# A recurrence with a top-2 mixture of experts: routing in two groups of twelve tiles instead of three of eight

## The chip, the core and the metric

One Trainium2 chip; the kernel runs on one core of it. The time is that of one execution on the device in microseconds (us). Before the change: 607.7 us, the median of three runs (606.4 to 608.46). The core has five engines that run their own instruction queues in order: TensorE (PE, with its weight loads PEld), VectorE (DVE), ScalarE (ACT), GpSimd (POOL) and SyncE (SP, here the queue that issues most DMAs).

## The reference

```python
# 1. recurrence per batch (4) and head (8), 768 steps, 48 dims
for t in range(S):
    cur = einsum('bhd,bhe->bhde', u[None] * kt, vt)
    y[:, :, t] = einsum('bhd,bhde->bhe', rt, state + cur)
    state = w[None, :, :, None] * state + einsum('bhd,bhe->bhde', kt, vt)
# 2. x: [3072 tokens, 384]; gate
noisy = x @ w_gate + log1p(exp(x @ w_noise)) * noise          # [3072, 8]
top2  = the two largest of each row; weights = softmax over the two
# 3. eight experts, 384 -> 1024 -> 384, float32
out[mask] += top2_w * (maximum(x[mask] @ w1[e], 0) @ w2[e])
```

## The kernel before, in words

**Stage 1, the recurrence ("attention"), 24 tiles.** A tile i is 128 tokens of one batch. For each tile, SP loads k, r and v (192 KB each, 1,024 rows of 192 bytes), POOL multiplies k by its decay table and makes r*k*u, PE turns k and r (`turn_kr`), multiplies them (`scores`), DVE masks the result (`mask`, L450), PE makes the output (`yout`, L496), and DVE adds the u term (`xout`, L522). That add, one per tile, is called x(i) below; it ends a tile. SP then writes x to DRAM (`xd`), from where experts gather their tokens by row. SP's queue is in order: the write of x(i) stands ahead of the loads of k and r for tile i+6, and those are issued five tiles ahead of use (`load(i + 5, (0, 2))`). Into the same loop go the loads of the noise (`load_nz`, four, 24 KB each in rows of 32 bytes, iterations 1 to 4) and the weights of expert 0 (seven units, three of 512 KB and four of 384 KB, at the iterations of the table `W_LD`), each of which ACT and DVE then split into a high and a low part (L344 to L349).

**Routing.** The gate of a group of tiles is worked out by `route(g)`, a generator of some sixty small DVE steps: softplus by polynomials, top-2 by two maxima, ranks within the experts by PE (L771 to L774), gate weights (written to `xd` as extra columns, L802), and then the list of expert 0's tokens. The lists are made by PE: `drop` builds two one-hot matrices on DVE (`r_oa`, `r_ob`), `place` multiplies them (L661), `placed` adds the result to `L`; `rows` turns it into row numbers `GR` (L819 to L821), by which POOL gathers (`xgather`, L956). Groups are 8 tiles. In the tile loop `steps(n)` takes n steps of the oldest generator at fixed places of each iteration, seven in all; so an order written out by hand decides which routing step stands where in DVE's queue. After the loop `rstep(us)` does the same between matmuls, with a credit in us.

**Stage 2, the experts.** Each expert has 832 token slots, seven tiles t (the last of 64 rows). Experts 1 to 7 take them in two chunks, tiles 0 to 2 (384 rows) and 3 to 6 (448 rows). `p1` makes the hidden layer (eight blocks f of nine matmuls, float32 in three products of high and low parts, L1053; ACT and DVE write `hb`), `p2` the output tile by tile (24 matmuls each, L1087). Expert 0 starts while routing is not finished, in three chunks: tiles 0 and 1 (256 rows) hold tokens of the first eight tiles only, tiles 2 and 3 those of the next eight, tiles 4 to 6 the rest. So the list of the first chunk is made in the tile loop (`early(0)`, at iteration 21), that of the second while PE works on the first (`list_01`, `early(1)`), and so on; the transposes of a chunk's gathered rows (`xT`, L979) stand in PE's queue inside `p2` of the chunk before it. Expert 1 needs all three groups (`list_1`), whose lists are made during expert 0's last chunk.

The change touches the tables at L47 and L48, L81, L84, L90, L92, `uterm_b` and `uterm_c`, `logits_out`, `drop`, `route`, `xT_first` (the first chunk's transposes), `list_01` and the code from L1243 on that puts the pieces in order.

Of the kernel before, what the change touches and what calls it, by code (L numbers as in the profile page):

```python
# [46 lines left out]
W_LD = {1: 0, 3: 1, 5: 2, 7: 3, 9: 4, 14: 5, 17: 6}  # L47
W_AT0 = (4, 6, 8, 10, 12, 17, 20)  # L48
# [3 lines left out]
def kernel(  # L52
# [519 lines left out]
    PS = rtp[0].tile([128, 5 * GB * E], F32, name="PS", bufs=1)  # L572
# [58 lines left out]
    def drop(g, mm2, ej2, ijv, w_, c0, first):  # L631

        i0, i1 = GROUPS[g]
        n = i1 - i0
# [9 lines left out]
        sh = [128, n, wp_ // 2, 2]
        o0, o1 = (ob[:, :, a].rearrange("p n (a b) -> p n a b", b=2) for a in range(2))
        nc.vector.tensor_tensor(o1, ej2[:, :, None, :].to_broadcast(sh),
                                ijv.rearrange("p (a b) -> p a b", b=2)[:, None].to_broadcast(sh), op=ALU.is_equal)
        yield c
        nc.vector.tensor_mul(o0, o1, thi[:, i0:i1, None, :].to_broadcast(sh))
        yield c  # L650
        pL = RT[:, 6 * GB * E:6 * GB * E + 2 * wp_].rearrange("p (a b) -> p a b", a=2)
# [910 lines left out]
```

## Time and profile before

| | |
|---|---|
| median of three runs | 607.7 us (606.4 to 608.46) |
| the profiled execution: its own time | 609.36 us |
| its span, first to last instruction | 607.5 us |
| mean granted TensorE clock | 0.981 of full speed |
| busy: PE / DVE / ACT / POOL | 94% / 59% / 47% / 45% |

The profile is of one execution. A row of the timeline has the start in us, the duration, the engine, the line, the operation with output and inputs, and in brackets how long the engine was idle before it and what ended that. "Chain" means the chain of work that ended last, followed back from the last instruction. The tile loop runs to about 126.8 us, expert 0 from there to 212.0 us, experts 1 to 7 to the end.

### The profile page before, as it was taken

How to read it: one execution, taken by the hardware profiler on the slowest of the kernel's cores; microseconds unless marked ns; L12 is line 12 of the kernel's file. 1: busy time of each engine (PE TensorE's matmuls, PEld its weight loads, DVE VectorE, ACT ScalarE, POOL GpSimd, SP SyncE). 2: the span in 40 equal slices, each digit the busy share in tenths (PEclk: the TensorE clock that was granted, in tenths of full speed). 3: DMA queues.
4: the chain of work that ended last, by engine and by line, in shares of the span. 5: the costliest groups of instructions: out<-in, count | busy, mean ns of one | idle time of the engine just before them, and what ended most of it. 6: DMA issues, size and time to landing. Idle time of an engine off the chain costs nothing.

```text
span 607.5 us, 13778 instructions
## 1 busy us (share of the span) xinstructions
PE 570.6 (94%) x5281; PEld 544.4 (90%) x5282; DVE 360.0 (59%) x866; ACT 284.4 (47%) x721; POOL 271.3 (45%) x420
## 2 busy tenths in 40 slices
PE   7898999884969999999999999999999999999995
PEld 4897889784959899999999999999999999999995
DVE  6997999974856574455554635564555636455331
ACT  4356788740234262544545454555445454445220
POOL 8978878601020655236442543245243426343222
PEclk9899999998979999999999999999999999999999
DMA  9989989365040564657647455664545554634211
GB/s 147 205 182 224 218 200 212 99 208 161 2 139 1 182 201 129 139 174 153 177 119 182 129 151 175 101 203 112 172 117 170 143 164 145 130 106 82 65 34 42
DMA packets 143018, 86.47 MB, mean 142 GB/s; under 512 B 118415, under 2 KB 133006, under 8 KB 142944
## 3 DMA queue, kind: packets, MB, share of 16 engines
q1 hardware_dynamic: 132384, 56.67, 40.1%
q0 software_dynamic: 9936, 28.83, 15.4%
q8 instruction: 44, 0.72, 0.5%
q14 instruction: 30, 0.25, 0.1%
q10 hardware_dynamic: 624, 0.00, 0.1%
HBM read 58.83 MB, written 19.76 MB: 129 GB/s over the span
## 4 chain that ended last, share of the span: by engine, by line
PE 77%; DVE 10%; DMA 6%; POOL 3%; issue 2%; ACT 1%; SPq 0%; POOLq 0%; DVEq 0%; ACTq 0%
PE ph L1053 35%; PE pym L1087 30%; PE py L496 2%; PE pym L1078 2%; PE pym L1080 2%; DVE am L450 2%; DMA kt<-in_k_dram 1%; PE PAB L442 1%; DMA vt<-in_v_dram 1%; DMA xg<-xd,GR 1%; PE KX L217 1%; DVE x L522 1%; PE ptm L979 1%; DMA out_dram<-ot,TK 1%; DMA stg<-in_moe_w_dram 1%
## 5 line engine op out<-in xcount | busy, mean ns | idle before, releaser
L1087 PE MATMUL pym<-w1h,hb 128*128 128x384 f32 x768 | 203.3, 342 | 0.0
L1087 PEld LDWEIGHTS pym<-w1h,hb 128*128 128x128 f32 x768 | 141.8, 191 | 0.2
L1057 DVE SCALAR_TENSOR_TENSOR hb<-ph,hb 128x384 fp32r<-128x384 f32 (+1 forms) x136 | 72.4, 532 | 117.1 <-ACT ht L1055 73.0
L1053 PE MATMUL ph<-xh,w0h 128*128 128x384 f32 (+3 forms) x408 | 140.0, 344 | 1.2 <-ACT xh L996 0.6
L1053 PE MATMUL ph<-xh,w0l 128*128 128x384 f32 (+3 forms) x408 | 138.8, 341 | 0.0
L1053 PE MATMUL ph<-xl,w0h 128*128 128x384 f32 (+3 forms) x408 | 133.5, 341 | 0.0
L1087 PE MATMUL pym<-w1l,hb 128*128 128x384 f32 x384 | 130.9, 341 | 0.0
L1055 ACT ACTIVATE hb<-ph 128x384 fp32r<-128x384 f32 (+1 forms) x136 | 64.3, 473 | 107.7 <-PE ph L1053 107.7
L1110 POOL DMA_INDIRECT out_dram<-ot,TK x56 | 57.9, 1034 | 107.7 <-DVE ot L1106 58.1
L956 POOL DMA_INDIRECT xg<-xd,GR x56 | 59.7, 1066 | 92.4 <-DVE r1r L560 27.5
L1053 PEld LDWEIGHTS ph<-xh,w0h 128*128 128x128 f32 x408 | 76.7, 188 | 4.7 <-ACT xh L996 0.7
L1053 PEld LDWEIGHTS ph<-xh,w0l 128*128 128x128 f32 x408 | 76.7, 188 | 2.6
L1053 PEld LDWEIGHTS ph<-xl,w0h 128*128 128x128 f32 x408 | 76.1, 188 | 2.8
L1087 PEld LDWEIGHTS pym<-w1l,hb 128*128 128x128 f32 x384 | 73.1, 190 | 0.1
L965 POOL DMA_INDIRECT pv<-out_dram,GA x49 | 49.7, 1014 | 47.8 <-DMA out_dram<-ot,TK 35.4
L1027 ACT ACTIVATE xh<-xj 128x384 fp32r<-128x384 f32 (+1 forms) x42 | 21.1, 502 | 43.5 <-DVE xj L1025 43.1
L1095 ACT ACTIVATE ot<-pym 128x384 f32<-128x384 f32 x39 | 19.0, 487 | 39.0 <-PE pym L1087 32.3
L1028 DVE TENSOR_TENSOR xl<-xj,xh 128x384 fp32r<-128x384 f32 (+1 forms) x42 | 22.4, 534 | 24.8 <-ACT xh L1027 24.8
L1013 ACT ACTIVATE pl<-xg 128x768 uint16<-128x768 uint16 (+1 forms) x42 | 35.3, 841 | 0.2 <-DMA xd<-pl 0.2
L391 POOL TENSOR_TENSOR kd<-kt,tabk 128x192 f32<-128x192 f32 x46 | 27.5, 621 | 10.6 <-DMA kt<-in_k_dram 6.2
L450 DVE TENSOR_TENSOR am<-PAB,mneg 128x512 int32<-128x512 int32 x48 | 30.7, 680 | 2.3 <-PE PAB L442 2.1
L419 ACT ACTIVATE cv<-vt,c 128x48 f32<-128x48 f32 x120 | 30.2, 323 | 0.3
(272 smaller groups left out, 826.4 us busy)
## 6 DMA issues: line engine op xcount, KB each, us to landing
stg<-in_moe_w_dram SPq DMA_DIRECT2D x24, 512.0 KB, 4.7
stg<-in_moe_w_dram SPq DMA_DIRECT2D x32, 384.0 KB, 3.4
rd<-in_r_dram SPq DMA_DIRECT2D x24, 192.0 KB, 4.4
vt<-in_v_dram SPq DMA_DIRECT2D x24, 192.0 KB, 4.3
xd<-x SPq DMA_DIRECT2D x24, 192.0 KB, 4.0
out_dram<-ot SPq DMA_DIRECT2D x16, 288.0 KB, 4.1
kt<-in_k_dram SPq DMA_DIRECT2D x23, 192.0 KB, 4.2
xg<-xd,GR POOLq DMA_INDIRECT x56, 3.1
```

The source lines that it names most:

```text
L391: nc.gpsimd.tensor_mul(KD[i][:, h], kt[i][:, h], tabk[:, h, :D])
L419: nc.scalar.activation(CV[i][:, h, :], vt[i][:, h, :], AF.Copy, scale=C8[i][:, h, :])
L450: nc.vector.tensor_tensor(am[:, :, h].bitcast(I32), pa[:, :, h].bitcast(I32), mneg[:, None].to_broadcast([128, 2, NP // 2, 128]), op=ALU.b ...
L956: nc.gpsimd.indirect_dma_start(out=xg[:n], out_offset=None, in_=xd[:rows_of(early_)], in_offset=bass.IndirectOffsetOnAxis(ap=GR[:n, e * NJ ...
L965: nc.gpsimd.indirect_dma_start(out=pv[:n], out_offset=None, in_=out, in_offset=bass.IndirectOffsetOnAxis(ap=GA[:n, e * NJ + t:e * NJ + t + ...
L1013: nc.scalar.activation(pl[:n], XG[e, t][:n, :DM].bitcast(U16).rearrange("p (d two) -> p two d", two=2), AF.Copy)
L1028: nc.vector.tensor_sub(xl, xj, xh.bitcast(F32))
L1053: nc.tensor.matmul(ph[:, :w_], a[:, d, fs], x[:, d, :w_], start=(j == 0), stop=(j == len(q) - 1))
L1055: nc.scalar.activation(h_[:, f, 0, :], ph[:, a:b], AF.Relu)
L1057: nc.vector.scalar_tensor_tensor(h_[:, f, 1, :], ph[:, a:b], 0.0, h_[:, f, 0, :].bitcast(F32), op0=ALU.max, op1=ALU.subtract)
L1087: nc.tensor.matmul(py, hb[:, f, a, hs], x[:, f, :], start=(j == 0), stop=(j == len(q) - 1))
L1110: st = nc.gpsimd.indirect_dma_start(out=out, out_offset=bass.IndirectOffsetOnAxis(ap=TK[:n, q:q + 1], axis=0), in_=ot[:n], in_offset=None, ...
```

## The change

Groups are 12 tiles, two of them. Expert 0's chunks are those of the other experts; its first chunk (384 rows) holds tokens of the first twelve tiles. Group 0 is routed in iterations 12 to 22 of the tile loop, and its list and gather come after x(22) (`I_EARLY`, moved behind `xout`). Group 1 is routed during `p1` and `p2` of expert 0's first chunk; `list_01` is gone. `drop` works in pieces of six tiles (`GD`). The noise is loaded in iterations 5 to 8 and the weight units in iterations 3, 5, ..., 15. The steps per iteration stay seven, with one moved (`steps(3)` behind the mask and none of `list_01`).

```diff
-W_LD = {1: 0, 3: 1, 5: 2, 7: 3, 9: 4, 14: 5, 17: 6}
-W_AT0 = (4, 6, 8, 10, 12, 17, 20)
+W_LD = {3: 0, 5: 1, 7: 2, 9: 3, 11: 4, 13: 5, 15: 6}
+W_AT0 = (6, 8, 10, 12, 14, 16, 18)
+NZ_AT = 5
+CV_DVE = 8
+GD = 6
...
-    CHUNKS0 = ((0, 1), (2, 3), (4, 5, 6))
+    CHUNKS0 = ((0, 1, 2), (3, 4, 5, 6))
...
-    EARLY = (0, 256, 512)
+    EARLY = (0, 384)
...
-    GROUPS = ((0, 8), (8, 16), (16, 24))
+    GROUPS = ((0, 12), (12, 24))
...
-    I_EARLY = 21
+    I_EARLY = 22
...
     def drop(g, mm2, ej2, ijv, w_, c0, first):
...
+        n = GD
+        for j0 in range(0, i1 - i0, n):
+            js = slice(j0, j0 + n)
+            oa = rtp[0].tile([128, n, 128], BF16, name="r_oa", bufs=2)
...
+            late_mm.append([2, lambda oa=oa, ob=ob: place(n, oa, ob, pL),
+                            lambda ob=ob: nc.scalar.activation(ob[:, :, 1], ob[:, :, 1], AF.Copy, scale=pcol),
+                            lambda f=first and j0 == 0: placed(pL, w_, c0, f), False])
...
-        ts = list(zip(chunks(0)[0], (RV, PAB)))
-        for t, dst in ts:
+        whole = RT[:, :ND * 128].rearrange("p (d t) -> p d t", d=ND)
+        ts = []
+        for t, dst in zip(chunks(0)[0], (RV, PAB, None)):
             for d in range(ND):
-                turn_rows(dst, d * 64, XG[0, t][:, d * 128:(d + 1) * 128])
...
+                xg = XG[0, t][:, d * 128:(d + 1) * 128]
+                if dst is None:
+                    nc.tensor.transpose(whole[:, d, :], xg, ident)
...
-    def list_01():
-        while late_mm:
-            yield "wait"
-        early(1)
-        yield 0.6
...
-        if i == I_EARLY:
-            while 0 not in routed or late_mm:
-                rstep(1)
-            early(0)
...
-        if 1 <= i <= B:
-            load_nz(i - 1)
+        if NZ_AT <= i < NZ_AT + B:
+            load_nz(i - NZ_AT)
...
         xout(i)
+        if i == I_EARLY:
+            while 0 not in routed or late_mm:
+                rstep(1)
+            early(0)
...
             mask(i + 1)
-            steps(2)
+            steps(3)
...
-    step, xt = stepper(STEPS_P2 / 3, 0, 1, (4, 5))
-    for t in p2(0, 0, step):
...
-    route_q.extend([list_0(), rest(0), rest(1), rest(2), list_1()])
-    for _ in p1(0, 1):
-        rstep(STEPS_P1)
-    while 2 not in routed:
+    route_q.extend([list_0(), rest(0), rest(1), list_1()])
+    step, xt = stepper(STEPS_P2 / 3, 0, 1, (6, 7, 8, 9))
+    for t in p2(0, 0, step):
+        hold.append((0, t))
...
+    while 1 not in routed:
         rstep(1)
...
-    step, xt = stepper(STEPS_R, 0, 2, (4, 5, 6))
-    for t in p2(0, 1, step):
```

How it moves instructions, at three places. First SP's queue behind the write of x(0) (`xd<-x`), where `kt`, `rd` and `vt` are the loads of k, r and v, `nz` the noise and `stg` a unit of weights. Before:

```order
L524 DMA xd<-x 128x384
L152 DMA kt<-in_k_dram 128x8x48
L152 DMA rd_102<-in_r_dram 128x8x48
L169 DMA nz<-in_moe_noise_dram 128x6x8
L152 DMA vt<-in_v_dram 128x8x48
L524 DMA xd<-x 128x384
L338 DMA stg<-in_moe_w_dram 128x1024
L152 DMA kt<-in_k_dram 128x8x48
L152 DMA rd_103<-in_r_dram 128x8x48
L169 DMA nz<-in_moe_noise_dram 128x6x8
L152 DMA vt<-in_v_dram 128x8x48
L524 DMA xd<-x 128x384
```

And now:

```order
L527 DMA xd<-x 128x384
L155 DMA kt<-in_k_dram 128x8x48
L155 DMA rd_102<-in_r_dram 128x8x48
L155 DMA vt<-in_v_dram 128x8x48
L527 DMA xd<-x 128x384
L155 DMA kt<-in_k_dram 128x8x48
L155 DMA rd_103<-in_r_dram 128x8x48
L155 DMA vt<-in_v_dram 128x8x48
L527 DMA xd<-x 128x384
L155 DMA kt<-in_k_dram 128x8x48
L155 DMA rd_104<-in_r_dram 128x8x48
L155 DMA vt<-in_v_dram 128x8x48
```

The first unit of weights and two loads of noise that stood here are gone from this piece; they come back later in the queue, beside the loads of later tiles.

Then POOL's queue at the end of the tile loop, where `kd`, `rku` are products of the recurrence and `xg<-xd` the gathers of expert 0's rows. Before:

```order
L402 TENSOR_TENSOR rku<-rku,ub 128x192 x2
L391 TENSOR_TENSOR kd_101<-kt,tabk 128x4x48 x2
L398 TENSOR_TENSOR rku<-rd_106,kt 128x192 x2
L402 TENSOR_TENSOR rku<-rku,ub 128x192 x2
L956 DMA xg<-xd,GR 128x392 x2
L398 TENSOR_TENSOR rku<-rd_107,kt 128x192 x2
L402 TENSOR_TENSOR rku<-rku,ub 128x192 x2
L956 DMA xg<-xd,GR 128x392 x4
L956 DMA xg<-xd,GR 64x392
L956 DMA xg<-xd,GR 128x392 x3
```

And now:

```order
L394 TENSOR_TENSOR kd_101<-kt,tabk 128x4x48 x2
L401 TENSOR_TENSOR rku<-rd_106,kt 128x192 x2
L405 TENSOR_TENSOR rku<-rku,ub 128x192 x2
L401 TENSOR_TENSOR rku<-rd_107,kt 128x192 x2
L405 TENSOR_TENSOR rku<-rku,ub 128x192 x2
L963 DMA xg<-xd,GR 128x392 x6
L963 DMA xg<-xd,GR 64x392
L963 DMA xg<-xd,GR 128x392 x3
L1123 MEMSET spacer 1x1
```

Two gathers that stood ahead of the products of the last tile now are three, behind them; with the next four they print as one row of six and one of 64 rows.

Last, DVE's queue from x(22) (the first row) on, where `am` is the mask of tile 23, `r_` and `RT` are routing, `L`, `lt` and `GR` a list. Before:

```order
L522 TENSOR_TENSOR x<-py,cv 128x384
L565 SCALAR_TENSOR_TENSOR RT<-RT,r1r 128x64
L450 TENSOR_TENSOR am<-PAB,mneg 128x2x256 x2
L567 SCALAR_TENSOR_TENSOR RT<-RT,r1s 128x64
L711 TENSOR_SCALAR RT<-RT 128x64
L349 TENSOR_TENSOR w1l_1122<-stg,w1h_1121 128x384
L713 RECIPROCAL r_d<-RT 128x64
L715 TENSOR_TENSOR r_s<-RT,r_d 128x64
L717 TENSOR_TENSOR r_s_2868<-r_s 128x64
L718 SCALAR_TENSOR_TENSOR r_sn<-r_s,nz 128x64
L522 TENSOR_TENSOR x<-py,cv 128x384
```

And now:

```order
L525 TENSOR_TENSOR x<-py,cv 128x384
L673 COPY L<-RT 128x2x7
L653 TENSOR_TENSOR r_ob<-r_pe_2703,ij 128x6x8
L656 TENSOR_TENSOR r_ob<-r_ob,thi 128x6x8
L675 TENSOR_TENSOR L<-L,RT 128x2x7
L826 SCALAR_TENSOR_TENSOR lt<-L 128x3
L827 TENSOR_SCALAR lt<-lt 128x3
L828 TENSOR_SCALAR GR<-lt 128x3
L453 TENSOR_TENSOR am<-PAB,mneg 128x2x256 x2
L525 TENSOR_TENSOR x<-py,cv 128x384
```

Where the second group's polynomials stood, the first group's list is finished; it stands ahead of the mask of the last tile.

## Rows read from the trace of the kernel before

**Rows 1.** Stretches: us, busy us of each engine, granted clock, DMA share, GB/s
```profile
36.62:78.44 41.82, 37.24 (x939) 34.56 (x939) 36.60 (x90) 28.27 (x89) 33.77 (x59) 1.00 0.97 215
78.44:121.27 42.83, 39.62 (x992) 36.82 (x988) 40.94 (x113) 33.79 (x120) 33.70 (x58) 1.00 0.75 171
121.27:126.82 5.55, 3.62 (x84) 3.04 (x85) 4.71 (x14) 3.35 (x15) 0.00 (x0) 1.00 0.14 50
126.82:212.02 85.20, 70.30 (x496) 66.57 (x497) 52.16 (x215) 25.12 (x69) 14.46 (x20) 0.90 0.40 120
212.02:600.50 388.48, 388.48 (x2141) 376.96 (x2140) 195.49 (x372) 178.94 (x395) 156.18 (x207) 1.00 0.51 137
```

**Rows 2.** Chain that ended last, whole span: start us, us, what
```profile
37.77 4.21 DMA kt<-in_k_dram
...
128.65 7.68 PE ph L1053 x63
...
151.46 2.56 PE pym L1087 x8
...
225.20 4.19 PE pym L1087 x24
...
268.71 12.64 PE ph L1053 x72
...
294.07 14.69 PE ph L1053 x72
```

**Rows 3.** Timeline of TensorE, 126 to 214 us
```profile
150.56 0.90 PE L979 MATMUL ptm<-ident,xg 128*128 128x128 f32 x3 [7.85 <-DMA xg<-xd,GR]
...
162.79 0.19 PE L774 MATMUL RT<-acc,ones_b 128*128 128x64 bf16 x1
...
175.34 0.87 PE L979 MATMUL ptm<-ident,xg 128*128 128x128 f32 x3 [3.20 <-DMA xg<-xd,GR]
...
185.75 0.42 PE L1053 MATMUL ph<-xh,w0h 128*128 128x320 f32 x1 [0.42 <-ACT xh L980]
...
198.21 0.34 PE L1087 MATMUL pym<-w1h,hb 128*128 128x384 f32 x1
...
208.93 0.44 PE L1078 MATMUL pym<-w1h,ht 128*128 128x384 f32 x1 [0.99 <-ACT ot L1093]
```

**Rows 4.** Stretches around the first wait of expert 0
```profile
147.00:150.50 3.50, 0.00 (x0) 0.00 (x0) 0.30 (x2) 0.00 (x0) 1.93 (x2) 0.54 0.27 67
...
154.00:156.00 2.00, 2.00 (x15) 2.00 (x14) 0.92 (x4) 0.68 (x3) 0.00 (x0) 0.97 0.00 0
```

**Rows 5.** Timeline of VectorE and GpSimd: a list and its gathers
```profile
114.78 0.17 DVE L821 TENSOR_SCALAR GR<-lt 128x2 int32<-128x2 f32 x1
...
115.25 1.15 POOL L956 DMA_INDIRECT xg<-xd,GR  x1 [3.05 <-DVE RT L553]
116.70 0.96 POOL L956 DMA_INDIRECT xg<-xd,GR  x1 [0.31 <-issue]
...
121.27 0.55 DVE L522 TENSOR_TENSOR x<-py,cv 128x384 f32<-128x384 f32 x1
...
171.96 1.24 POOL L956 DMA_INDIRECT xg<-xd,GR  x1 [22.28 <-DMA stg<-in_moe_w_dram]
```

**Rows 6.** Groups by form, VectorE, 58 to 215 us: busy us, mean ns
```profile
L640 DVE TENSOR_TENSOR r_oa<-r_dm,im 128x1024 bf16<-128x1024 bf16 x6 | 4.1, 688 | 1.6 <-PE RT L661 1.5
...
L565 DVE SCALAR_TENSOR_TENSOR RT<-RT,r1r 128x64 f32<-128x64 f32 x10 | 2.2, 224 | 0.1
...
L565 DVE SCALAR_TENSOR_TENSOR RT<-RT,r2r 128x8 f32<-128x8 f32 x10 | 1.7, 172 | 0.3
...
L713 DVE RECIPROCAL r_d<-RT 128x64 f32<-128x64 f32 x2 | 1.1, 548 | 0.0
```

**Rows 7.** DMA queue q1 of two stretches, 0 to 20 and 130 to 142 us: packets, MB, share
```profile
q1 hardware_dynamic: 17698, 3.18, 102.4%
...
q1 hardware_dynamic: 2540, 3.61, 97.4%
```

More of the change, by code (lines that the diff above doesn't have):

```diff
@@ L537, in logits_out @@
         if j == 0:
-            to_moe = g == 2 and att_pool[0] is att
-            LG[g] = (moe if to_moe else att_pool[0]).tile([128, GB, 2 * E], F32, name="lg", bufs=1 if to_moe else 2)
+            to_moe = g == len(GROUPS) - 1 and att_pool[0] is att
+            LG[g] = (moe if to_moe else att_pool[0]).tile([128, GB, 2 * E], F32, name="lg", bufs=1)
         nc.scalar.activation(LG[g][:, j, :], PL[i][:, 0, :], AF.Copy)
@@ L571 @@
     RT = psum.tile([128, 512], F32, name="RT", tag="rt")
-    PS = rtp[0].tile([128, 5 * GB * E], F32, name="PS", bufs=1)
+    PS = rtp[0].tile([128, 4 * GB * E], F32, name="PS", bufs=1)
     PG = [RT]
@@ L644, in drop @@
[L644 to L651, printed above, removed]
@@ L1331, in stepper @@
         return f, x
-    step, xt = stepper(STEPS_P2 / 3, 0, 1, (4, 5))
-    for t in p2(0, 0, step):
-        hold.append((0, t))
-    for _ in xt:
-        pass
     def list_0():
@@ L1341, in list_0 @@
             yield "wait"
-        rows(EARLY[2] // 128, NJ)
-        xgather(0, 2)
+        rows(EARLY[1] // 128, NJ)
+        xgather(0, 1)
         yield 0.6
@@ L1366 @@
         wstep()
-    step, xt = stepper(STEPS_R, 0, 2, (4, 5, 6))
-    for t in p2(0, 1, step):
-        hold.append((0, t))
-        wstep()
-        wstep()
-    for _ in xt:
-        pass
-    for s in range(2, len(seq)):
+    for s in range(1, len(seq)):
         e, ci = seq[s]
         end = s + 1 == len(seq)
-        if s == 3:
+        if s == 2:
             nxt = w_split(2)
             wq.extend(nxt[:ND])
-        elif s == 4:
+        elif s == 3:
             NLAG[0] = 1
@@ L1385 @@
             lows = []
-        if s > 3:
+        if s > 2:
             xh_, xj_ = xD(*seq[s + 1]) if not end else ([], [])
@@ L1390 @@
         for j, _ in enumerate(p1(e, ci)):
-            while hold and (s > 2 or listed):
+            while hold and (s > 1 or listed):
                 emit_out(*hold.pop(0))
-            if s == 2:
+            if s == 1:
                 rstep(STEPS_L0)
@@ L1396 @@
                 continue
-            if s > 3:
-                if xh_ and j in ((3, 4, 6) if s == 4 else ((0, 1, 3, 4), (0, 2, 4))[ci]):
+            if s > 2:
+                if xh_ and j in ((3, 4, 6) if s == 3 else ((0, 1, 3, 4), (0, 2, 4))[ci]):
                     xh_.pop(0)()
-                if s == 4:
+                if s == 3:
                     wstep()
@@ L1432, in step_x @@
             at[0] += 1
-            if at[0] in (XJ_AT if s > 4 else (2, 4, 6)) and xj_:
+            if at[0] in (XJ_AT if s > 3 else (2, 4, 6)) and xj_:
                 xj_.pop(0)()
@@ L1442, in step_x @@
                 lows.append(un)
-        for t in p2(e, ci, step_x if s > 3 else step_02 if s == 2 else None):
-            if s > 3 and tw(t) < 128:
+        for t in p2(e, ci, step_x if s > 2 else step_02 if s == 1 else None):
+            if s > 2 and tw(t) < 128:
                 step_x()
-            if s == 3:
+            if s == 2:
                 next(xt, None)
                 if t == 1:
-                    xgather(*seq[5])
-            if s < 4:
+                    xgather(*seq[4])
+            if s < 3:
                 wstep()
@@ L1462 @@
                 pass
-        while s > 3 and (xj_ or lows):
+        while s > 2 and (xj_ or lows):
             if xj_:
```

75 lines of the change are left out of this document (42 added, 33 removed).

## The prediction, made before the changed kernel ran

> **What bounds the kernel now.** I read the stretches first, then the chain of waits, then the timelines of TensorE, VectorE and GpSimd where the chain leaves TensorE, and the DMA queue of the first 20 us. Four things are to be seen.
>
> From 212.02 us on TensorE is never idle: 388.48 of 388.48 us [rows 1]. A chunk of 384 rows costs 12.64 us in its first layer, one of 448 rows 14.69 us [rows 2], so 0.1756 and 0.204 us per matmul; a full tile of the second layer costs 4.19 us (24 matmuls). A whole expert is 388.48 / 7 = 55.5 us. Nothing after expert 0 is touched, so it only starts earlier or later.
>
> Expert 0 takes 85.20 us with TensorE busy for 70.30 of them at a mean clock of 0.90 [rows 1], some 30 us more than another expert. The waits are in front of the transposes of its second and third chunks, 7.85 and 3.20 us [rows 3]: the list of the next eight tiles was not ready.
>
> In the second half of the tile loop, from x(13) at 78.44 to x(22) at 121.27 us, VectorE is busy for 40.94 of 42.83 us: it is the bound. From x(5) to x(13) the DMA share is 0.97 over 41.82 us, and VectorE has 36.60 [rows 1]: there transfers bind, VectorE close behind. At 37.77 us the chain stands in a load of k for 4.21 us [rows 2].
>
> From x(22) to the first expert matmul it is 5.55 us [rows 1], with no wait for a gather: the list for it was done at 114.95 and its gathers started at 115.25 and 116.70 us [rows 5].
>
> **The change, part by part.** The sum is made against the profiled execution, 609.36 us (span 607.5), which lies 1.7 above the median of 607.7.
>
> A1, later noise and weights, to x(13). One load of k, r or v is 1,024 packets; 17,698 packets went in the 18 us in which the queue ran at the start [rows 7], so 1.04 us each. Four noise loads have 768 packets each: 0.8 us. Bulk writes run at 3.61 MB in 12 us, 301 GB/s [rows 7], so a 512 KB unit is 1.7 and a 384 KB unit 1.3 us. Ahead of the load of k that landed at 41.98 us three noise loads and one unit go away: 4.1 us less. But all of it comes back: by the loads that x(13) needs, only one 384 KB unit is still ahead of its old place, 1.3 us. What tiles 10 to 13 also lose is the first group's routing on VectorE (in the order 32 instructions beside a tile's own before, five now). So the gain at x(13) is at least that 1.3 us if transfers bind throughout, and at most about 5, if nothing but TensorE's busy time (37.24 of 41.82 us [rows 1]) were left. I take 3, nearer to the transfers, since their share is 0.97. That sets x(13) at 75.4.
>
> A2, tiles 14 to 22. Beside the fixed instructions of a tile (routing and the split of weights), the order has 60 on VectorE between x(13) and x(22) before and 72 now, since all of group 0's routing falls here. Twelve more at 0.224 us are 2.7 us. About 38 work on 96 columns instead of 64; a 64-wide step is 0.224 and an 8-wide one 0.172 us [rows 6], 0.05 us for 56 columns, so 0.03 us more each, 1.1 us. The reciprocal goes from 0.548 to some 0.8. Building a one-hot (0.688 us for eight tiles) takes two of three quarters. Together 4.3 us on an engine with 1.9 us idle in that stretch. I take +3.5; from 0 (all of it in gaps) to +5.5 (more conflicts with POOL). x(22) comes at 121.8, +0.5.
>
> A3, from x(22) to the first matmul. The first list now ends behind x(22): copy, two one-hot products, ACT's scaling, six placements on PE, add, three list steps. By steps of 0.17 to 0.22 us [rows 6] on VectorE, and as much again for ACT and PE between them, I estimate 2.8 us to `GR`, and the mask of tile 23 waits behind it on VectorE. POOL starts 0.3 us later (as 114.95 to 115.25). Three gathers, not two, start about 1.4 us apart (115.25 to 116.70); the third transposes 3.4 us after its start (171.96 to 175.34 [rows 3, 5]). So the last tile of rows is on PE at 2.8 + 0.3 + 2.7 + 3.1 to 3.4, about 9; with 0.9 for its transposes (as at 150.56) and some 0.5 until ACT has copied them (0.42 at 185.75 [rows 3]) the first matmul stands at x(22) + 10.5 instead of + 5.55: +5. The cover (a whole tile and more between list and use) is gone, and nothing else hides it. Bounds: +3.5 if the gathers overlap well, +6.5 if the lists wait for PE. The first expert matmul then comes at 132.3, +5.5.
>
> B, expert 0, counted from its first matmul. First layer 72 x 0.1756 = 12.65; the last tile's gate logits stand in it as before, 0.7 (126.82 to 128.65 less nine matmuls of 0.122 [rows 1, 2]): 13.35. Then 40 matmuls of the second layer, 7.0: 20.4. The rank matmuls, estimated at 0.6: 21.0. From there to the transposes of the next chunk the third group took 162.98 to 175.34 = 12.4 us [rows 3]; now the pieces are longer (two one-hots of six tiles) but three hidden-layer evictions fewer stand in between, so 12.2: 33.2. Only 8 of the 32 matmuls left lie under that wait; PE idles for about 10.5 us, in place of 7.85 + 3.20 and some smaller ones. Then 24 matmuls and four transposes, the first eight at the lower clock (2.56 us [rows 2] instead of 1.40) and with placements between them: 8.3, so 41.5. First layer of 448 rows, 14.7, with six placements in between; the old third chunk took 12.46 us (185.75 to 198.21) for 72 matmuls of 320 rows (by its neighbours 0.149 each, 10.7) and four placements of eight, so 0.44 each; six of six tiles about 2.3: 58.5. Second layer: 3 x 4.19, three sets of transposes at half of 0.9, 1.4, the 64-row tile 16 x 0.1756 = 2.8: 75.3. The wait for an output buffer at 208.93 (0.99 us [rows 3]) goes, since its scatter is issued about 4 us before the tile that needs it ends. Add 1.2 for a slow start (below): 76.5 instead of 85.2: -8.7. Little of it is arithmetic: a 256-row matmul costs 0.122 us (63 in 7.68 [rows 2]), so the first layer was 17.6 + 10.7 = 28.3 us and is 27.35; the rest is one wait for two, and blocks at half clock. Bounds: -11 (the lists come 2 us sooner) to -5 (the wait grows by 3 us).
>
> C, the rest: 0.
>
> The slow start: when TensorE stood idle from 142.7 us, the granted clock fell to half within the stretch that begins at 147.0, and stayed there until about 154, well after work began at 150.56 [rows 4]; eight matmuls then took 2.56 us [rows 2]. Before the change TensorE had nearly no gap ahead of its first expert matmul; now it has about 5 us with three short bursts of transposes. I count one such block, 1.2 us. The Trainium skill (TensorE: Matmul & The Clock Gate, Part 1: The HAM clock gate) says that the array is throttled to 1.2 GHz by default and that activity releases it, so a gap is paid twice. By that rule the sum is as given; were the clock kept, it would be 1.2 us lower. The trace agrees with it after the first wait.
>
> Sum: -3.0 + 3.5 + 5.0 - 8.7 = -3.2 us: 606.2 for the profiled execution, 604.5 for the median; with the slow start perhaps longer than one block I say 605.
>
> **The rivals.**
>
> R1, slower: the start of expert 0 slips by more than expert 0 gains. Mechanism: group 0's whole routing and list sit on VectorE, the engine that already has 40.94 of 42.83 us, and the gathers come last. With A1 at -1.3, A2 at +5.5, A3 at +6 the first matmul comes 10.2 us late; expert 0 gains 7 to 8.7: +2 to +3, 610. It decides when the first expert matmul stands later than 126.82 + 8.7 = 135.5 us. For it: the busy share. Against: the routing that leaves tiles 10 to 13, and 1.9 us of idle time.
>
> R2, much faster: transfers were what held tiles 6 to 13 and the routing steps fall into gaps. A1 -5, A2 +1, A3 +5, B -9: -8, so 600. For it: the 4.21 us wait in the chain at 37.77 and a share of 0.97. Against: the same bytes must go before x(13) but for one unit.
>
> R3, no change: the wait before the second chunk grows, as one list of twelve tiles must be made under 384 rows of work, where before 512 rows of work lay over the same steps in two lists. If the list comes 3 us later, B is -5.5 and the sum is 0: 607.7. In the same case falls that "loaded later" is only half true: the last unit is loaded in iteration 15 now, 17 before.
>
> **How the numbers follow.** The forecast has 0.40, R1 0.24, R2 0.18, R3 0.18. The likeliest one's own range is 602 to 607. The ends of the terms add up to -12.5 and +5.7, 595 to 613; that all fall to one side is unlikely, so 598 to 612 holds R1, R2 and R3 and leaves out some 0.2. What a measurement of this kernel tells from no change is about 0.3%, 1.8 us. Faster by that (below 605.9): three quarters of the forecast and all of R2 and a little of R3, 0.51. Within it: a sixth of the forecast and most of R3, 0.23. Slower: R1 and the rest, 0.26.
>
> **What would show it.** A1: x(13) near 75.4, and no wait of POOL for k before tile 8. A2: x(22) between 120 and 124 and VectorE busy for over 95% from x(13) on. A3: ACT or PE waiting for `xg<-xd` ahead of the first `ph` matmul, about 10 us after x(22). B: one wait of 9 to 12 us in front of the `ptm` transposes, none in front of a third set; first matmul of expert 1 about 77 us after the first of expert 0. The prediction is wrong if x(22) moves by more than 3 us, or if the single wait is shorter than 7 or longer than 14 us.

## The result, and the profile after

The changed kernel takes 601.45 us (median of 4 runs, 598.46 to 602.99) where the kernel before, on the same chip, took 607.77. The ratio is 0.9893, 95% interval 0.9851 to 0.9935: faster by 1.1%, some 6.3 us. Run again as `e1_after_again` beside other runs of the kernel before, it came to 0.9819 (0.9775 to 0.9862). The forecast was 605.0 in 598 to 612. Both medians lie in that range, but below the 602 to 607 that the forecast gave as the likeliest.

The profiled execution has a span of 596.7 us, in place of 607.5: 10.8 us less, so it is a quick one of its kind. The stretches, cut at the same events as before [rows 1], with `x(5)`, `x(13)` and `x(22)` now at 36.11, 72.13 and 117.81 us, the first expert matmul at 127.63 and expert 1 at 204.70:

```profile
36.11:72.13 36.02, 34.62 (x931) 33.60 (x931) 30.92 (x60) 27.40 (x88) 33.21 (x57) 1.00 0.95 212
72.13:117.81 45.68, 40.08 (x987) 36.87 (x981) 44.63 (x124) 35.01 (x123) 32.07 (x57) 1.00 0.71 167
117.81:127.63 9.82, 7.11 (x109) 6.28 (x109) 4.54 (x15) 4.28 (x17) 3.06 (x3) 0.78 0.41 123
127.63:204.70 77.07, 65.80 (x412) 60.93 (x412) 45.63 (x164) 23.35 (x62) 14.83 (x20) 0.92 0.41 126
204.70:596.70 392.00, 385.76 (x2142) 375.57 (x2141) 196.13 (x373) 178.72 (x395) 157.98 (x207) 1.00 0.50 136
```

The order is length, then busy time of PE, PEld, DVE, ACT and POOL, clock, DMA share, GB/s. In the second row VectorE has 44.63 of 45.68 us: nearly all routing of twelve tiles and the first part of the list stand there. The last row surprises: seven experts that the change does not touch take 392.0 us and not 395.5 (607.5 - 212.02).

In expert 0 the waits of TensorE are now these (start, duration, in brackets the idle time before it and what ended it); before there were 7.85 us ahead of one set of `ptm` transposes and 3.20 ahead of another [rows 3]:

```profile
154.89 0.31 PE L667 MATMUL RT<-r_ob,r_oa 128*128 128x16 bf16 x6 [3.57 <-ACT r_ob L659]
156.46 0.33 PE L667 MATMUL RT<-r_ob,r_oa 128*128 128x16 bf16 x6 [1.26 <-DVE L L675]
161.25 0.90 PE L986 MATMUL ptm<-ident,xg 128*128 128x128 f32 x3 [4.47 <-DMA xg<-xd,GR]
...
187.21 0.42 PE L667 MATMUL RT<-r_ob,r_oa 128*128 128x100 bf16 x6 [1.13 <-ACT r_ob L659]
...
192.55 0.55 PE L986 MATMUL ptm<-ident,xg 128*128 128x128 f32 x3 [0.69 <-DMA xg<-xd,GR]
```

One wait in three pieces, 3.57 + 1.26 + 4.47 = 9.3 us, in place of two: list, placements, gather. The same path now also stands ahead of the first expert matmul. GpSimd now waits 8.34 us for the list `GR`, which VectorE writes at 120.10 us, and issues three gathers behind x(22) (117.81):

```profile
120.56 1.15 POOL L963 DMA_INDIRECT xg<-xd,GR  x1 [8.34 <-DVE GR L828]
122.02 0.96 POOL L963 DMA_INDIRECT xg<-xd,GR  x1 [0.31 <-issue]
123.29 0.95 POOL L963 DMA_INDIRECT xg<-xd,GR  x1 [0.31 <-issue]
```

There were two before, and they started at 115.25 and 116.70 [rows 5], 6 and 4.6 us ahead of x(22).

The seven experts, from the chain of work that ended last (start, duration, what): first of the kernel before, then of the changed one. `ph` is the first layer of a chunk, `pym` x72 three full tiles of the second. Expert 2 begins at 268.71 and 261.20, expert 3 at 324.31 and 316.27; [rows 2] has the first two `ph` rows of before.

```profile
281.35 12.72 PE pym L1087 x72
...
308.76 12.72 PE pym L1087 x72
324.31 12.50 PE ph L1053 x72
336.81 12.51 PE pym L1087 x72
349.31 14.71 PE ph L1053 x72
```

```profile
261.20 12.63 PE ph L1067 x72
273.83 12.48 PE pym L1101 x72
286.31 14.68 PE ph L1067 x72
300.99 12.48 PE pym L1101 x72
316.27 12.48 PE ph L1067 x72
...
341.23 14.41 PE ph L1067 x72
```

The same 72 matmuls of the same shape take 12.72 us in an even expert and 12.51 in an odd one before, and 12.48 in the rows of both now; a 448-row first layer of an odd expert took 14.71 and takes 14.41. An even expert is 55.07 us long in place of 55.60, an odd one 54.67 in place of 55.01.

### The profile page after: what moved, and what is told of

It reads as the page before. It is cut to its first block, busy times and chain, and to the rows that moved or that the text cites. A ratio compares the mean times of both kernels' runs of the same rounds, so it can differ in the third digit from the quotient of the medians.

```text
span 596.7 us, 13551 instructions
## 1 busy us (share of the span) xinstructions
PE 564.5 (95%) x5207; PEld 539.7 (90%) x5208; DVE 350.8 (59%) x798; ACT 283.3 (47%) x716; POOL 273.6 (46%) x420
## 4 chain that ended last, share of the span: by engine, by line
PE 70%; issue 6%; DMA 1%; DVE 1%; POOL 0%; POOLq 0%; ACT 0%
PE ph L1067 34%; PE pym L1101 31%; PE pym L1094 2%; PE pym L1092 2%; DMA xg<-xd,GR 1%; PE ptm L986 1%; PE RT L667 0%; POOL xg L963 0%; DVE r_oa L648 0%; DVE xl L988 0%; POOL out_dram L1124 0%; DVE r_ob L656 0%; DVE ot L1120 0%; POOLq L1481 0%; DVE r_ob L653 0%
## 5 line engine op out<-in xcount | busy, mean ns | idle before, releaser
L1101 PE MATMUL pym<-w1h,hb 128*128 128x384 f32 x768 | 200.2, 337 | 0.0
L1071 DVE SCALAR_TENSOR_TENSOR hb<-ph,hb 128x384 fp32r<-128x384 f32 x128 | 71.2, 556 | 119.3 <-ACT ht L1069 71.4
L1067 PE MATMUL ph<-xh,w0h 128*128 128x384 f32 (+1 forms) x384 | 136.2, 355 | 0.1
L1067 PE MATMUL ph<-xh,w0l 128*128 128x384 f32 (+1 forms) x384 | 135.3, 352 | 0.0
L1067 PE MATMUL ph<-xl,w0h 128*128 128x384 f32 (+1 forms) x384 | 129.7, 351 | 0.1
L1069 ACT ACTIVATE hb<-ph 128x384 fp32r<-128x384 f32 x128 | 62.9, 492 | 105.6 <-PE ph L1067 101.8
L1124 POOL DMA_INDIRECT out_dram<-ot,TK x56 | 60.8, 1086 | 98.5 <-DVE ot L1120 46.8
L1067 PEld LDWEIGHTS ph<-xh,w0h 128*128 128x128 f32 x384 | 72.5, 189 | 3.2 <-ACT xh L1010 0.3
L1067 PEld LDWEIGHTS ph<-xl,w0h 128*128 128x128 f32 x384 | 72.2, 189 | 3.1 <-DVE xl L988 0.5
L1067 PEld LDWEIGHTS ph<-xh,w0l 128*128 128x128 f32 x384 | 72.5, 189 | 2.6
```

What stands on the lines that cost most here:

```text
L1067: nc.tensor.matmul(ph[:, :w_], a[:, d, fs], x[:, d, :w_], start=(j == 0), stop=(j == len(q) - 1))
L1069: nc.scalar.activation(h_[:, f, 0, :], ph[:, a:b], AF.Relu)
L1071: nc.vector.scalar_tensor_tensor(h_[:, f, 1, :], ph[:, a:b], 0.0, h_[:, f, 0, :].bitcast(F32), op0=ALU.max, op1=ALU.subtract)
L1101: nc.tensor.matmul(py, hb[:, f, a, hs], x[:, f, :], start=(j == 0), stop=(j == len(q) - 1))
L1124: st = nc.gpsimd.indirect_dma_start(out=out, out_offset=bass.IndirectOffsetOnAxis(ap=TK[:n, q:q + 1], axis=0), in_=ot[:n], in_offset=None, ...
```

## The experiments

The twelve runs ran in three groups, each beside its own runs of the kernel before: e1 to e4 (median of the kernel before 609.86 us), e8 to e11 (610.82), and e5, e14, e17 and e18 (609.39), the last group on another chip than the first two. Ratios are to these medians, with 95% intervals. "x(13)" and so on are read from the timelines of the profiles.

**e1_after_again: is it the kernel or the execution?** No edit.

> The changed kernel once more, unaltered, for a second profile. In the first one x(13) starts at 72.13 us (78.44 before), the first expert matmul at 127.63, expert 1 at 204.70, and the seven other experts take 392.0 us in place of 388.5+; that is 54.9 us an expert where 55.5 were measured before. Theory 1 (the start is a property of the new order of loads, the pace of one execution): x(13) again between 71 and 73.5 us, expert 0 at 77 +/- 1 us, but the seven other experts anywhere from 391 to 395 us; time 600 to 603. Theory 2 (the faster experts belong to the kernel): 54.9 us an expert again, 392 +/- 0.5 us. Theory 3 (x(13) at 72.13 was a lucky execution): x(13) at 74 to 76 and expert 1 about 3 us later, as forecast.

Ratio 0.9819 (0.9775 to 0.9862). x(13) at 71.92 us, expert 0 77.6 us, seven experts 391.9 us: both differences came again, so theory 2 on the experts, and theory 1's place for x(13). It did not stay there: in e9 and e11 below, whose work up to x(13) is the same, x(13) stood at 75.64 and 76.03 us.

**e2_loads_early, e18_loads_early_again: are the later loads what brought x(13) forward?**

```diff
-W_LD = {3: 0, 5: 1, 7: 2, 9: 3, 11: 4, 13: 5, 15: 6}
-W_AT0 = (6, 8, 10, 12, 14, 16, 18)
-NZ_AT = 5
+W_LD = {1: 0, 3: 1, 5: 2, 7: 3, 9: 4, 14: 5, 17: 6}
+W_AT0 = (4, 6, 8, 10, 12, 17, 20)
+NZ_AT = 1
```

> The changed kernel with the first weights and the noise loaded as early as before, everything else as changed. Theory (transfers set the pace up to x(13), and the bytes moved behind it are gained in full): x(13) goes from 72.1 back to 76 to 78 us, the part from x(13) to x(22), bound by VectorE, keeps its 45.7 us, so x(22) is at 122 to 124, and the time is +3 to +6 us over the changed kernel. Rival 1 (what brought x(13) forward is the routing work that left tiles 10 to 13, not the loads): x(13) stays at 72 to 74, time 0 to +1.5. Rival 2 (the loads matter up to x(8) only and are given back, as the forecast had it): x(13) +1.3 to +3, time +1 to +3.

> The changed kernel with the early loads of before, a second time, beside the kernel before with late loads. Up to x(9) its program is that of the kernel before. Theory (the 55.7 us at x(9) was an execution with quick transfers; from x(9) on the two groups save 2 to 3 us): x(9) at 57 to 59, x(13) at 74.5 to 77. Rival (early loads cost next to nothing with two groups): x(9) at 55 to 56.5, x(13) at 72 to 73.5. In both the time is 600 to 604, 6 to 10 us below the kernel before.

Measured: x(13) at 72.81 and 74.75 us, x(22) at 117.07 and 119.18 (x(13) to x(22) 44.3 and 44.4 us, less than the 45.7 with late loads, of which one more unit is split there). Ratios 0.9833 (0.9794 to 0.9871) and 0.9905 (0.9888 to 0.9921), within what the two intervals of the changed kernel span, 0.9775 to 0.9935. My theory of the first expectation fell, and its rival 1 came: x(13) did not go back to 76 to 78. In the second run x(9) came at 57.25, not at 55.72 as in the first, as its theory had it: same program, other execution, and another chip.

The later loads do move x(9). It stands at 53.6 to 56.1 us in the six profiles with late weights and noise, and at 55.7 to 59.5 in the seven with both early, on average 3.2 us sooner. At x(13) little of that lead is left: 73.3 us on average against the 72.81 and 74.75 here.

**e5_before_late: later weight loads alone.**

```diff
-W_LD = {1: 0, 3: 1, 5: 2, 7: 3, 9: 4, 14: 5, 17: 6}
-W_AT0 = (4, 6, 8, 10, 12, 17, 20)
+W_LD = {3: 0, 5: 1, 7: 2, 9: 3, 11: 4, 13: 5, 15: 6}
+W_AT0 = (6, 8, 10, 12, 14, 16, 18)
```

> The kernel before with the first weights loaded as late as in the changed kernel (the noise stays early). Up to now x(13) stood at 78.4, 79.7 and 78.4 us with the early loads and three groups, at 72.8 with early loads and two groups, and at 71.8 to 76.0 with late loads and two groups. Theory (the regrouping brings x(13) forward, the loads next to nothing): x(13) at 77 to 79, time within 1.5 us of the kernel before. Rival (the later loads bring 3 us or more and the run with early loads was a lucky one): x(13) at 73 to 76, time -2 to -4.

Ratio 1.0004 (0.9984 to 1.0025); x(9) at 56.98, x(13) at 77.60, x(22) at 121.89, as the theory had it. The later weight loads are worth nothing in the time, with three groups as with two. (In the kernel before's two profiles, and in e10 and e17, which add only an unused tile to it, x(13) stands at 78.44, 79.74, 78.36 and 77.64.) What the later noise does by itself no run shows.

**e14_route_later: routing out of tiles 10 to 13, alone.** Kernel before, first group routed four tiles later.

```diff
-            if b == i + 1:
+            if b + (4 if g == 0 else 0) == i + 1:
```

> The kernel before with the routing of its first group begun four tiles later (behind tile 11's logits in place of tile 7's); loads, groups and chunks as before. Some 24 routing instructions of VectorE leave tiles 10 to 13. Up to x(9) the program is the kernel before's, so x(9) is at 58 to 59.5 us if the three profiles so far are typical, and at 55.7 if the run with two groups and early loads (the same program up to there) was. Theory (routing in tiles 10 to 13 delays x(13)): x(9) to x(13) takes 17 to 18 us in place of 20 to 20.3, and x(13) to x(22) gets back at least that, since the same steps now stand there and 33 of them in one lump ahead of x(21): time 0 to +4 against the kernel before. Rival (transfers bind there, routing hides in the waits): x(9) to x(13) 20 us again.

Ratio 1.0033 (1.0017 to 1.0049). x(9) to x(13) took 19.93 us: the rival. Here is that stretch in the kernel before, in this run and in e18, columns as above:

```profile
58.17:78.44 20.27, 18.10 (x452) 16.60 (x452) 20.00 (x57) 16.02 (x56) 17.06 (x31) 1.00 0.98 218
```

```profile
57.21:77.14 19.93, 17.84 (x456) 16.75 (x456) 15.74 (x30) 16.11 (x56) 17.65 (x31) 1.00 0.96 219
```

```profile
57.25:74.75 17.50, 16.38 (x434) 15.72 (x436) 16.07 (x30) 15.71 (x55) 16.95 (x30) 1.00 1.00 231
```

Before, VectorE is busy for 20.00 of 20.27 us: it binds. With the routing out of the way it has 15.74, and x(13) came no sooner for it. From 36 to 78 us GpSimd waited 5.2 us for `kt` in this run, 2.4 in e18 and 0.2 in e2; up to x(13) the three have nearly the same instructions (VectorE's differ in the width of one and the place of one mask), and x(13) stood at 77.14, 74.75 and 72.81. Of those 5.2 us only 1.1 lie in the stretch shown, beside 1.2 in which GpSimd waited for TensorE. So my reading, which no run isolates, is that the regrouping takes a bound away that hid another, the loads; what lies beneath is 4.3 us wide over these three executions. The routing that was moved was paid later: x(13) to x(22) took 48.87 us in place of 42.83.

**e3_list_sooner: the list for the first chunk a tile earlier.**

```diff
-    I_EARLY = 22
+    I_EARLY = 21
-            steps(3)
+            steps(5)
```

> The changed kernel with group 0's routing taken five steps at a time behind each mask in place of three, and its list begun one tile sooner, so that the list is done right behind x(21) and the three gathers start about 3 to 4 us sooner. Theory (between x(22) and the first expert matmul the path is list, three gathers, transposes): the first expert matmul comes 5 to 6 us after x(22) in place of 9.8, x(22) 0 to 1 us later since VectorE does the same work in the same time; time -3 to -4.5 us. Rival (VectorE is full from x(13) to x(22), so each routing step taken sooner puts x(22) and x(23) later by its own time): x(22) +2 to +4 us, the first expert matmul where it was, time within 1 us.

Ratio 0.9862 (0.9817 to 0.9906), median 602.97 against 599.95 for e1, with intervals that overlap: not faster. x(21) at 117.71 us and x(22) at 126.25 (113.83 and 118.10 in e1), first expert matmul at 132.95, 4.7 us later than in e1. Neither theory came in full. The routing taken sooner put x(21) 3.9 us later, by the rival's mechanism (VectorE is full), so that the list, though it now follows x(21), was written at 119.36 in place of 120.10 in the first profile of the changed kernel, only 0.7 us sooner. And the gathers now stood in GpSimd's queue ahead of the products of tile 23, which neither had foreseen. First GpSimd, then VectorE:

```profile
110.33 1.14 POOL L405 TENSOR_TENSOR rku<-rku,ub 128x192 f32<-128x192 f32 x2
119.82 1.15 POOL L963 DMA_INDIRECT xg<-xd,GR  x1 [8.36 <-DVE GR L828]
...
123.52 1.15 POOL L401 TENSOR_TENSOR rku<-rd,kt 128x192 f32<-128x192 f32 x2
124.61 1.13 POOL L405 TENSOR_TENSOR rku<-rku,ub 128x192 f32<-128x192 f32 x2
```

```profile
117.71 0.56 DVE L525 TENSOR_TENSOR x<-py,cv 128x384 f32<-128x384 f32 x1 [0.45 <-ACT r_ob L659]
...
125.78 0.55 DVE L413 TENSOR_REDUCE c<-rku 128x8 f32<-128x384 f32 x1 [4.09 <-POOL rku L405]
126.25 0.55 DVE L525 TENSOR_TENSOR x<-py,cv 128x384 f32<-128x384 f32 x1
```

GpSimd stood for 8.36 us at a gather whose list was not there, with two products behind it that were ready, and VectorE then waited 4.09 us for them ahead of x(22). The changed kernel also has the 8.34 us of waiting, but with no product behind it.

**e4_more_cover: more of the second layer under the wait.**

```diff
-    step, xt = stepper(STEPS_P2 / 3, 0, 1, (6, 7, 8, 9))
+    step, xt = stepper(STEPS_P2 / 3, 0, 1, (9,))
```

> The changed kernel with the transposes and placements of expert 0's second chunk behind all of the first chunk's second layer in place of behind its second tile: 32 matmuls lie under the wait for the rows in place of 8. Theory (the single wait in front of the transposes ends when the list and gathers are done, whatever TensorE does meanwhile): the wait of 3.6 + 1.3 + 4.5 us in front of them shrinks by 24 matmuls, 4.2 us, less 1 to 1.5 us for transposes whose eviction is now exposed in front of the first layer; expert 0 at 74 to 75 us in place of 77.1, time -2 to -3. Rival (the placements and evictions that were spread between those 24 matmuls now stand bare in front of the first layer, and matmuls of the wait run at half clock): what is gained under the wait is given back, expert 0 at 76.5 to 78, time within 1 us.

Ratio 0.9881 (0.984 to 0.9922), 602.67 us: 2.7 over e1, with intervals that overlap; expert 0 took 79.7 us, 77.6 in e1. Neither forecast came: the rival's mechanism did, and cost more than it said. The theory's first half held: from the first expert matmul to the first layer of the second chunk it is 37.58 us, 41.92 in e1. But from there to expert 1 it is 42.11 in place of 35.70. The time under the wait had not been lost: the routing of the last lists ran in it on VectorE, and now the placements that followed stood bare before the second layer (TensorE's timeline, then a stretch of it, columns as above):

```profile
185.12 0.42 PE L667 MATMUL RT<-r_ob,r_oa 128*128 128x100 bf16 x6 [1.12 <-ACT r_ob L659]
186.37 0.44 PE L667 MATMUL RT<-r_ob,r_oa 128*128 128x100 bf16 x6 [0.82 <-DVE L L675]
187.60 0.66 PE L667 MATMUL RT<-r_ob,r_oa 128*128 128x100 bf16 x6 [0.80 <-DVE r_oa L648]
188.86 0.66 PE L667 MATMUL RT<-r_ob,r_oa 128*128 128x100 bf16 x6 [0.60 <-ACT r_ob L659]
189.30 0.67 PE L1101 MATMUL pym<-w1h,hb 128*128 128x384 f32 x1
189.77 0.52 PE L1101 MATMUL pym<-w1l,hb 128*128 128x384 f32 x1
190.09 0.84 PE L1101 MATMUL pym<-w1h,hb 128*128 128x384 f32 x2
```

```profile
189.30:194.00 4.70, 4.70 (x18) 4.70 (x16) 2.18 (x12) 0.00 (x0) 2.02 (x3) 0.51 0.16 46
```

Between 185.12 and 189.30 TensorE did little, and the next matmuls stand 0.32 us apart (189.77 to 190.09) where 0.174 is their full pace, until about 194 us: the granted clock was 0.51 there. The tie of these two (that the routing would have been done under the longer wait) is read from the traces; no run took it apart.

**e8_before_again: the kernel before a second time.** No edit, one execution.

> The kernel before once more, unaltered, for a second profile. In the first one x(5) to x(13) takes 41.82 us; the changed kernel took 36.0 and 35.4, and with its loads put back to the old places still 36.3. In that first profile a packet of 192 bytes took 16 to 19 ns in the first 40 us, in all the others 15. Theory 1 (the 36 us belong to the regrouping: routing steps that left tiles 8 to 13): x(5) to x(13) at 41 to 42.5 us again, x(13) at 77.5 to 79.5. Theory 2 (the first profile of the kernel before had slow transfers, so part of the 6.3 us is that execution): x(5) to x(13) at 37 to 40 us, x(13) at 74 to 77. For the pace of experts: the seven others take 395.5 +/- 0.5 us again if it belongs to the kernel.

x(5) to x(13) took 41.98 us, seven experts 395.4: theory 1 in its number, though e14 showed that it named at most half the cause.

**e9_after_pad64: where do 3.5 us in untouched experts come from?** The changed kernel's routing tiles take 64 bytes per partition less, and all that is placed below them moves up by 64, among it the odd experts' weights from 139008 to 139072, the hidden layer `hb` from 188160 to 188224 (places in bytes, within a partition). One unused tile puts these back.

```diff
     PS = rtp[0].tile([128, 4 * GB * E], F32, name="PS", bufs=1)
+    rtp[0].tile([128, 16], F32, name="pad", bufs=1)
```

> The changed kernel with one unused tile of 64 bytes per partition in the routing's pool, which puts the odd experts' weights and the hidden layer (hb, ht) back to the very addresses that they have in the kernel before (139008 and 188160; the changed kernel has 139072 and 188224, since its routing tiles take 64 bytes less). No instruction is added. Theory (a matmul's pace hangs on where its stationary and moving tiles lie to each other; the 3.5 us that the seven experts gained come from those 64 bytes): full tiles of the second layer of even experts go from 12.48 to 12.72 us for three, the 448-row chunk of odd experts from 14.41 to 14.7, the seven experts take 395.2 +/- 0.5 us, time +3 to +3.5 over the changed kernel. Rival (the pace comes from the groups, the chunks or the DMA traffic of the changed kernel): 392.0 +/- 0.3, time the same.

Ratio 0.9955 (0.9921 to 0.9989): of the changed kernel's 1.1 to 1.8% less than half is left. Seven experts 395.2 us, and every phase at the old pace:

```profile
279.57 12.72 PE pym L1102 x72
...
347.54 14.71 PE ph L1068 x72
```

The theory holds for the pace: 64 unused bytes in on-chip memory cost 3.2 us in the seven experts. In the time the pad costs more than the 3 to 3.5 us that were expected: 607.89 us stand against 600.78 for e11 of the same group. The profiles of these two differ by 4.0 us, 3.8 of them in the seven experts; what made e9's other executions longer no trace shows. The pad moves the recurrence's tiles too, but x(13) does not follow that: 75.64 us here, 76.03 in e11, where they lie as in the changed kernel.

**e10_before_pad64 and e17_before_pad192: the same from the other side.** The kernel before, with `[128, 16]` and with `[128, 48]` in the same place.

```diff
     PS = rtp[0].tile([128, 5 * GB * E], F32, name="PS", bufs=1)
+    rtp[0].tile([128, 48], F32, name="pad", bufs=1)
```

> The kernel before with one unused tile of 64 bytes per partition in the routing's pool: odd experts' weights at 138944 and the hidden layer at 188096, which leave the same remainder by 128 as in the changed kernel. No instruction is added. Theory (the remainder by 128 of the two tiles to each other sets the pace): the seven experts take 392.2 +/- 0.5 us in place of 395.5, even experts' second layer 12.48 for three tiles in place of 12.72, odd experts' 448-row chunk 14.41 in place of 14.7; time -3 to -3.5 against the kernel before. Rival 1 (the exact addresses, or xh at 99040 in place of 98784, matter): 395.5, time the same. Rival 2 (the pace belongs to the changed order of work): 395.5, time the same.

> The kernel before with one unused tile of 192 bytes per partition in the routing's pool: odd experts' weights at 138816 and the hidden layer at 187968, which leave the same remainder by 256 (64) as in the changed kernel; the pad of 64 bytes left the same remainder by 128 alone, and was slower in the first layer. No instruction is added. Theory (remainders by 256 of stationary and moving tile set the pace): the seven experts take 392.1 +/- 0.4 us in place of 395.5: second layer of even experts 12.48 in place of 12.72, 448-row chunk of odd ones 14.41 in place of 14.7; time -3 to -3.5 against the kernel before. Rival (a larger distance counts, or what else differs in the changed kernel): the 448-row chunks stay at 14.7 and the seven experts take 394 or more.

With 64 bytes: ratio 0.9984 (0.9959 to 1.001), seven experts 398.4 us, which neither theory nor rivals had. The 2.9 us over the kernel before are all in expert 1 (59.6, 56.7 before), and there 2.2 are two waits of TensorE in the first layer, no matter of pace; the other six together are as long as before. Among them the second layer of even experts became quick, the first layer of odd ones slower than ever: the remainder by 128 alone is not it. With 192 bytes: ratio 0.994 (0.9913 to 0.9967), seven experts 392.0 us as forecast, every phase at the changed kernel's pace. First the pad of 64 (TensorE's two waits, then the chain), then that of 192:

```profile
219.07 0.44 PE L1054 MATMUL ph<-xh,w0h 128*128 128x384 f32 x1 [1.16 <-issue]
...
221.97 0.45 PE L1054 MATMUL ph<-xh,w0h 128*128 128x384 f32 x1 [1.06 <-DVE hb L1058]
```

```profile
285.48 12.48 PE pym L1088 x72
...
353.15 14.88 PE ph L1054 x72
```

```profile
279.79 12.48 PE pym L1088 x72
...
347.19 14.41 PE ph L1054 x72
```

So 0.6% of the time, about half of the change's gain as first measured, is to be had without the change. That remainders by 256 decide is what all placements tried agree with; a larger distance is not ruled out.

**e11_even_weights: a placement for the even experts too.** The changed kernel, with the even experts' weights 32 bytes lower (remainder 64 by 256, as the odd ones') and `xh` kept where it was.

```diff
+    moe.tile([128, 8], F32, name="pad", bufs=1)
-        tie = const.tile([1, 1], F32, name="tie")
+        tie_mx = const.tile([1, 2], F32, name="tm")
+        tie = tie_mx[:, 0:1]
-        mx = const.tile([1, 1], F32, name="mx")
+        mx = tie_mx[:, 1:2]
```

> The changed kernel with the even experts' weights 32 bytes lower (24384, remainder 64 by 128, as the odd experts' weights have it; two small tiles of the end share one), all other tiles of the experts where they were. In the changed kernel the odd experts run each phase at the fast pace (12.48, 12.48, 14.41 us), the even ones the first layer at a slower one (12.63 and 14.68 us). Theory (pace by remainders): the even experts' first layer goes to 12.48 and 14.41, 0.42 us an expert, 1.3 us in experts 2, 4 and 6 and up to 0.4 in expert 0; seven experts 390.7 +/- 0.3, time -1.3 to -1.7 against the changed kernel. Rival (even experts are slower for another reason, their weights being loaded and split at the time): 392.0, time the same.

The even experts' first layer goes to the quick pace; this is expert 2:

```profile
266.45 12.50 PE ph L1069 x72
278.95 12.48 PE pym L1103 x72
291.43 14.41 PE ph L1069 x72
```

An even expert takes 54.68 us in place of 55.07, so 1.2 us in three. The seven took 391.4, 0.7 more than forecast; 0.5 of it is the tail behind the last matmul, 6.7 us here and 6.2 in the changed kernel. The ratio, 0.9818 (0.9775 to 0.9861), is the same as e1's: 1 us is below what these runs tell apart. By its rows its experts are the quickest of all versions; that it beats the changed kernel in time is not shown.

## Why the prediction was right, and where not

Each term, as forecast, in the first pair of profiles, and in the pair e8 to e9, where the two kernels have the experts' tiles at the same remainders:

| term | forecast | before to after | e8 to e9 |
|---|---|---|---|
| A1, to x(13) | -3.0 | -6.3 | -4.1 |
| A2, x(13) to x(22) | +3.5 | +2.9 | +2.8 |
| A3, x(22) to first expert matmul | +5.0 | +4.3 | +4.7 |
| B, expert 0 | -8.7 | -8.1 | -7.3 |
| C, the rest | 0 | -3.5 | -0.2 |
| sum | -3.2 | -10.8 | -4.1 |

The time fell inside the range, but the forecast's size did not hold: -6.3 us, and some -11 in e1 (0.9819 of 609.86), stand where -3.2 was summed up. Two terms of the sum were too small, and both errors go the same way. The sign "x(22) moves by more than 3 us", named as one of being wrong, came in the first profile: 121.27 to 117.81, 3.5 us sooner, since A1 came at -6.3.

- **C failed**: "C, the rest: 0", and ahead of it "it only starts earlier or later". The instructions are the same, but the sizes of routing tiles moved the experts' tiles by 64 bytes, and a matmul's pace hangs on that. e9 takes the 3.5 us away but for 0.2, e17 gives them to the kernel before. What the change is worth without C is less sure. e9's ratio of 0.9955 is -2.7 us (-4.8 to -0.7), next to the forecast's -3.2, and the first measurement less 3.5 us is -2.8; but e1's less 3.5 is -7.5, near to R2. No run settles which.
- **A1 was mis-sized**, outside its bounds of -5 to -1.3 in this execution. Over the profiles x(13) stands at 78.5 us on average with three groups and early loads (four, 77.6 to 79.7) and at 73.3 with the change and the edits of it that keep its loads (six, 71.8 to 76.0): -5.2. The groups of runs differ too: between the profiles of e8 and e9, of one group, it is -4.1. The forecast took 3, "nearer to the transfers", by the share of 0.97. The runs put the weight elsewhere. With early loads and no routing in tiles 10 to 13, x(13) comes at 72.8 and 74.8 (two groups) and at 77.1 (e14), 74.9 on average; later weight loads with that routing in place reach only 77.6. So most of the gain goes with the routing that left, but these three lie 4.3 us apart, and no run isolates how much of it that is. VectorE's 20.00 of 20.27 us from x(9) on had been averaged away in the one stretch from x(5) to x(13) [rows 1], where it showed 36.60 of 41.82. That all bytes "come back" was right: the later loads bring x(9) 3.2 us forward, with no wait of GpSimd for k between 16 us and x(9) in the first profile, and next to none of it is left at x(13).
- **A2** was right in sign, place and about size: VectorE busy for 98% (44.63 of 45.68).
- **A3** was right: list, then gathers, then transposes, 9.82 us where 10.5 was worked out. TensorE waited for a gather in it, as the sign said:

```profile
125.74 0.40 PE L220 MATMUL PAB<-ident,xg 64*128 64x64 f32 x6 [1.02 <-DMA xg<-xd,GR]
```

  In e3 the list's steps were called sooner, and the list came only 0.7 us sooner. The first matmul stood at 127.63, well short of the 135.5 from which R1 would have decided, mostly since x(13) came early.
- **B** was right in its wait and its total: one wait of 9.3 us where 10.5 was forecast, no wait over 0.7 us ahead of the third set of transposes, expert 0 77.1 us where "about 77" was named as the sign. Its other pieces were not measured one by one.
- **R2** (600 us) has the time, and without C the terms of the first pair sum up to -7.2, near to its -8. But its mechanism was half of it: A1 went below -5, while the routing steps did not fall into gaps (A2 +2.9, not +1). That the time is R2's 600 owes 3.5 us to C, which no rival had. R3's longer wait did not come.
- **The slow start**, 1.2 us: ahead of expert 0's first layer it came in the first profile of the changed kernel, with a granted clock of 0.62 in the stretch around the first expert matmul (0.50, the 1.2 GHz level, from that matmul to 129.00), and in e1 it was over by then, 1.00 (changed kernel, then e1):

```profile
126.00:129.00 3.00, 2.66 (x19) 2.07 (x15) 1.35 (x3) 1.64 (x6) 0.00 (x0) 0.62 0.87 264
```

```profile
126.00:129.00 3.00, 2.32 (x25) 1.73 (x25) 2.13 (x4) 2.10 (x8) 0.00 (x0) 1.00 0.40 126
```

  In e1 the clock had been low earlier, 0.50 and 0.51 from 121 to 126 us and 0.66 on the mean from x(22) to that matmul, where the first profile has 0.78 in its third stretch. So it fell into B in the first profile and into A3 in e1. The Trainium skill (TensorE: Matmul & The Clock Gate, Part 1: The HAM clock gate) says that the throttled clock is the default and activity releases it; both profiles agree, as both had gaps ahead of these matmuls (1.48 and 1.49 us of idle TensorE in front of the last placements behind x(22)). Expert 0 was no shorter in e1 for it, 77.6 against 77.1 us: there the clock stayed at 0.50 longer behind the one wait, and from the first transposes to the first layer of the second chunk it took 9.24 us in place of 7.86.

## What to carry to other kernels

Where a change alters the size of any tile, compare the addresses of the tiles that the bound engine reads, before and after; a phase whose like instructions run at two paces (even and odd buffers, as here) is a hint that they matter, and an unused tile of some bytes tests it; look at what else that tile moves. Read the busy share tile by tile where the work changes within a stretch: the mean from x(5) to x(13) hid that VectorE took over at x(9). And before moving a wait's work elsewhere, look at what other engines do under it, and at what stands behind the waiting instruction in its queue.

## What the runs showed of the hardware that was not expected

- The pace of a matmul of one shape depends on where its stationary and moving tiles lie in on-chip memory: 173.3 or 176.7 ns for 384 columns (12.48 and 12.72 us for 72), 200.1, 204.3 or 206.7 for 448 (14.41, 14.71, 14.88 for 72). With the first layer's moving rows at remainder 224 by 256 in all placements, 448 columns were quick with weights at 64, slower at 0 and 96, slowest at 192; in the second layer, moving weights at 96 were slow with `hb` at 0 and quick with it at 64 or 192. Why, no run says.
- Executions of nearly the same instructions (e2, e18 and e14, the last two on another chip) reached x(13) at 72.81, 74.75 and 77.14 us, with waits of 0.2, 2.4 and 5.2 us for loads of k; the changed kernel and edits that leave its work up to x(13) alone reached it at 71.8 to 76.0. One profile of this stretch, whose DMA share is 0.95 and more, is one draw of several.
